# Squares turned by VectorE in the last batch, another tail and new orders of the steps: a fused attention and two-MoE kernel on one core

## The chip, the core and the metric

The kernel runs on one core of a Trainium2 chip. Its engines work side by side, each through its own queue in order: TensorE (PE: matmuls and transposes, its weight loads shown apart as PEld), VectorE (DVE), ScalarE (ACT), GpSimd (POOL) and SyncE (SP), which here issues all the transfers. The metric is the device time of one execution in microseconds.

## The reference

Three stages follow one another: attention with normalized queries and keys, a gated feed-forward layer, and a soft mixture of eight experts whose weights over tokens and slots come from the same logits.

```python
# attention: q, k, v of (4 batches, 12 heads, 448 tokens, 64)
q_n, k_n = rmsnorm(q, g_q), rmsnorm(k, g_k)
attn = softmax(q_n @ k_n.T / 8)
x = (attn @ v) as (1792 tokens, 768)
# gated layer, 768 -> 1536 -> 768
h = silu(x @ w_gate) * (x @ w_val)
x = h @ w_out
# soft mixture: phi (768, 32), 8 experts of 4 slots, hidden width 1024
logits = x @ phi
d = softmax(logits, over tokens);  c = softmax(logits, over slots)
slot_in = d.T @ x
slot_out[e] = relu(slot_in[e] @ w1[e]) @ w2[e]
return c @ slot_out
```

All is fp32. The rows of a token never meet those of another, but for the attention within a batch and the softmax over all 1792 tokens.

## The kernel before, in words

**Products in two parts.** A product of full accuracy is made of three faster ones: each operand is split into a high part (rounded, type fp32r) and a low part (what the rounding left), and high times high, high times low and low times high are summed. For the weights `w_hi` makes the high part on ScalarE and `w_lo` the low one (L239). Other products and all transposes stay fp32.

**Stages.** A hand-written schedule runs in steps `t`. In steps 0 to 27 (`step0`) the attention of batch 0 runs, with the preparation of the weights beside it: `w_out` times `phi` is folded into one matrix `wp`, so that the logits come straight from `h`, and the 24 blocks of `w_gate` and `w_val` are written back as fp32. From step 28 on (`step`, with `u = t - 28`) each step makes one product of 18 matmuls (`gv`, L615, in two halves `G0` and `G1`): even `u` a gate block, odd `u` the value block, so a pair gives one of the 12 blocks of 128 rows of `h` for a batch. The 24 steps of a batch carry the attention of the next batch with them; the last batch (`u` from 72 to 95) has no attention beside it.

**A block of `h`.** The gate goes through a tanh on ScalarE (`act_gate`), VectorE multiplies it (`act_gate_mul`, L636, then `act_val`, L642, with the value). The two products have one PSUM bank each (`g` and `v`), so a gate product can start only when the multiplication of the gate before has read its bank. Then the block is needed twice: as it is, for the logits (`logits`, `lp`, L679, summed by VectorE at L685, in the last batch for every two blocks), and with tokens on the partitions, for the slots. For that `h_trans` (L659) turns it on TensorE in four transposes of 112 tokens, and ScalarE copies the result from PSUM into `hn`.

**The end of a batch.** `slots1` sums the logits (`lt`) and makes them once more with tokens on the partitions (`ln`, L703 and L705, for `ce`); `slots2` takes the maximum and the exponential over tokens (`et`, with a running maximum over the batches); `slots3` turns `et` (`dp`, copied to `dn`), and `slots4` multiplies `dn` with `hn` (`sp`, L746) and adds to `acc`. For the last batch `slots4_last` goes on to the slots' inputs (`sip`).

**The experts.** From there the weights `w1` and `w2` of the experts stream through 15 buffers of 1.5 MB (`load_unit`); each unit of a load is consumed by 16 to 24 matmuls (`s` L1431 and `so` L1458). Loads wait in SP's queue for a buffer to come free; the first 11 are issued during the last batch. The last four units are ordered so that the left half of the 768 columns is ready first.

**The tail.** `combine1` to `combine3` make `c` (as `ct`, with high and low parts stacked, 96 rows). `slot_out` brings a half of the slots' outputs together: two copies out of PSUM, one matmul with a selecting matrix, a rounding and a subtraction (`sst`, 96 rows). `output` makes one matmul of 384 columns for 112 tokens (L1417) and one copy (L1419), VectorE and ScalarE by turns. `TO` says how many of the 16 output matmuls of the left half stand behind each of the last units: 8 before the right half's products, 8 between them.

**The order of a step** is written out as lists of names: `ORDA` for the first two steps, `ORD0` and `ORDB` for the rest of `step0`, `ORD1` for the first 24 of the later steps and `ORD2` for the others. `S` are the scores, `M0`/`M1` the maxima, `E0`/`E1` the exponentials, `P0`/`P1` the transposes of the probabilities and `V0`/`V1` their copies out of PSUM, `T`/`TH`/`L` the turning and splitting of queries and keys, `X` the product with `v`, `AT`/`AM` the activations, `HT` the turning of `h`, `LG` the logits, `W4` the split of the last batch's weights, `Z1` to `Z4` the `slots` functions. `fill(n)` issues 4n small matmuls on zeros, which keep TensorE at work (`warm_ps`, L115); `LF`, `TF` and `FILL` are their counts.

## Time and profile before

| | us |
|---|---|
| median of 3 runs | 833.52 |
| lowest and highest | 832.75, 835.16 |
| the profiled execution | 833.85 |
| its span | 832.1 |
| outside of the span | 1.75 |

The profile's page gives busy times by engine and the chain of waits that ended last: 60% of the span lies on TensorE, 33% in the products of L615, 6% in transfers of the experts' weights. TensorE's matmuls overlap: a product's matmul is shown with some 366 ns, and the next one starts 0.2 us later. What a group of matmuls costs is therefore read from the chain, where the time of a piece ends when the next one starts. Times on the left of a row are microseconds from the start of the span.

### The profile page before, as it was taken

The page shows a single profiled execution, that of the slowest core. Times are in us where ns is not written, and L with a number is a line of the kernel's source. Part 1 is how long each engine was busy: PE and PEld are TensorE (multiplying, and loading weights), DVE is VectorE, ACT ScalarE, POOL GpSimd, SP SyncE. Part 2 cuts the span into 40 slices and gives each one's busy share as a digit, 9 for nine tenths or more (in the row PEclk, how much of TensorE's full clock was granted, in tenths as well). Part 3 has the DMA queues.
Part 4 walks back from the last instruction along what each step waited for, and adds up shares of the span by engine and source line. Part 5 has one row for each costly group of instructions (what it writes and reads, how often), then busy time and mean ns, then how long its engine had stood idle before and what let it go on. Part 6 is the DMA issues. An engine that isn't in the chain of part 4 may idle for free.

```text
span 832.1 us, 14229 instructions
## 1 busy us (share of the span) xinstructions
PE 790.9 (95%) x5460; PEld 594.0 (71%) x5460; DVE 462.1 (56%) x777; ACT 439.3 (53%) x940; POOL 333.1 (40%) x327
## 2 busy tenths in 40 slices
PE   6799989999999999999999999999999999988685
PEld 5556657778778767787778677877878888555353
DVE  4879978777778555555556555545354344220013
ACT  3777877878678546556566455655333333220012
POOL 7987867675756543445444344322000000010000
PEclk8999999999999999999999999999999999999877
DMA  6566665765656312322223222221337778899997
GB/s 212 161 197 188 204 206 164 238 223 177 195 188 223 107 53 80 110 91 77 83 80 95 68 85 60 69 75 52 96 107 252 285 286 321 270 397 403 403 343 235
DMA packets 77891, 148.87 MB, mean 179 GB/s; under 512 B 5888, under 2 KB 48128, under 8 KB 77824
## 3 DMA queue, kind: packets, MB, share of 16 engines
q1 hardware_dynamic: 77824, 147.97, 53.5%
q8 instruction: 43, 0.70, 0.3%
q14 instruction: 24, 0.20, 0.1%
HBM read 128.29 MB, written 19.66 MB: 178 GB/s over the span
## 4 chain that ended last, share of the span: by engine, by line
PE 60%; DMA 6%; ACT 1%; POOL 1%; DVE 1%; issue 0%; SPq 0%; DVEq 0%; ACTq 0%; POOLq 0%
PE pg L615 33%; DMA w<-in_moe_w_dram 6%; PE tp L521 5%; PE xp L548 5%; PE s L442 3%; PE th L659 2%; PE so L1458 2%; PE sp L746 1%; PE lp L679 1%; PE tq L372 1%; PE s L446 1%; PE s L1417 1%; PE s L1431 1%; PE sip L800 0%; POOL pr L486 0%; PE ln L703 0%
## 5 line engine op out<-in xcount | busy, mean ns | idle before, releaser
L615 PE MATMUL pg<-xh,wh 128*128 128x448 f32 x576 | 222.5, 386 | 0.0
L615 PE MATMUL pg<-xl,wh 128*128 128x448 f32 x576 | 210.6, 366 | 0.0
L615 PE MATMUL pg<-xh,wl 128*128 128x448 f32 x432 | 157.9, 365 | 0.1
L457 DVE TENSOR_REDUCE sm<-s 128x1 f32<-128x448 f32 x168 | 100.5, 617 | 73.4 <-PE s L442 52.7
L469 ACT ACTIVATE pr<-s,sm 128x448 f32<-128x448 f32 x168 | 106.2, 639 | 63.5 <-DVE sm L457 61.1
L486 POOL TENSOR_SCALAR pr<-pr,su 128x448 f32<-128x448 f32 x84 | 70.9, 854 | 117.5 <-DVE su L482 106.0
L615 PEld LDWEIGHTS pg<-xh,wh 128*128 128x128 f32 x576 | 108.6, 189 | 12.4 <-issue 5.1
L615 PEld LDWEIGHTS pg<-xl,wh 128*128 128x128 f32 x576 | 108.9, 189 | 6.4
L521 PE MATMUL tp<-ident,pr 128*112 128x128 f32 x672 | 101.9, 280 | 4.3 <-ACT pt L535 2.1
L521 PEld LDWEIGHTS tp<-ident,pr 128*112 128x112 f32 x672 | 74.7, 135 | 38.2 <-issue 13.2
L231 ACT CAST wh<-raw 128x768 fp32r<-128x768 f32 x96 | 79.5, 830 | 29.0 <-PE pg L615 22.8
L239 DVE TENSOR_TENSOR wl<-raw,wh 128x768 fp32r<-128x768 f32 x72 | 81.0, 1124 | 11.2 <-ACT wh L231 11.2
L615 PEld LDWEIGHTS pg<-xh,wl 128*128 128x128 f32 x432 | 81.2, 188 | 7.2 <-DVE wl L239 0.5
L535 ACT COPY pt<-tp 112x512 f32<-112x512 f32 x130 | 74.0, 595 | 13.3 <-PE tp L521 7.4
L341 POOL TENSOR_TENSOR ri<-ss,mhalf 112x16 f32<-112x16 f32 (+1 forms) x25 | 70.1, 2805 | 2.1
L423 POOL CAST qz<-qa 64x128 fp32r<-64x128 f32 x48 | 35.1, 732 | 78.3 <-DVE qa L414 70.1
L442 PE MATMUL s<-ka,qa 64*128 64x448 f32 x432 | 63.6, 399 | 0.8 <-ACT qa L403 0.7
L660 ACT COPY hn<-th 112x512 f32<-112x512 f32 x48 | 28.4, 591 | 58.9 <-PE th L659 58.9
L548 PE MATMUL xp<-pt,vt 112*64 112x448 f32 x288 | 58.1, 546 | 0.0
L347 POOL TENSOR_TENSOR qn<-qk,ri 112x512 f32<-112x512 f32 x46 | 52.9, 1150 | 1.1
L615 PE MATMUL pg<-xh,raw 128*128 128x448 f32 x144 | 52.6, 366 | 0.0
L197 POOL TENSOR_SCALAR hpos<-r 128x768 uint16<-128x768 int16 x36 | 46.2, 1282 | 4.6 <-DMA r<-in_moe_w_gate_dram 1.7
(161 smaller groups left out, 1103.9 us busy)
## 6 DMA issues: line engine op xcount, KB each, us to landing
w<-in_moe_w_dram SPq DMA_DIRECT2D x25, 1536.0 KB, 10.6
raw<-w SPq DMA_DIRECT2D x72, 384.0 KB, 3.2
w<-raw SPq DMA_DIRECT2D x36, 384.0 KB, 2.9
r<-in_moe_w_out_dram SPq DMA_DIRECT2D x12, 768.0 KB, 5.1
r<-in_moe_w_gate_dram SPq DMA_DIRECT2D x12, 768.0 KB, 5.2
r<-in_moe_w_val_dram SPq DMA_DIRECT2D x12, 768.0 KB, 5.0
qk<-in_q_dram SPq DMA_DIRECT2D x24, 224.0 KB, 3.2
qk<-in_k_dram SPq DMA_DIRECT2D x24, 224.0 KB, 3.4
```

What stands on the lines that cost most here:

```text
L231: (nc.vector.tensor_copy if u - NO < NU and WH1 == "v" else nc.scalar.copy)(out=wh, in_=wst[u]["raw"])
L239: eng.tensor_tensor(out=wl, in0=wst[u]["raw"], in1=wst[u]["wh"].bitcast(F32), op=ALU.subtract)
L341: nc.gpsimd.tensor_tensor(out=ri, in0=ss, in1=mhalf[:, : len(ns)], op=ALU.pow)
L347: eng.tensor_tensor(out=st[i]["qn"][:, n].rearrange("p c h d -> p h c d"), in0=st[i]["qk"][:, n], in1=st[i]["ri"][:, n] .rearrange("p (h c ...
L442: nc.tensor.matmul(sc[j], qa[r, wt, c * P : (c + 1) * P], ka[r, mv, :], start=(n == 0), stop=(n == 2))
L457: nc.vector.tensor_reduce(out=d["sm"][:, j : j + 1], in_=d["sc"][j], axis=AX.X, op=ALU.max, negate=True)
L469: nc.scalar.activation(out=p, in_=d["sc"][j], func=AF.Exp, bias=d["sm"][:, j : j + 1], accum_out=st[i]["su"][:, c, j : j + 1])
L486: nc.gpsimd.tensor_scalar(out=p, in0=p, scalar1=su[:, j : j + 1], scalar2=1.0, op0=ALU.mult, op1=ALU.mult)
L521: nc.tensor.transpose(tp[:CP, ck * P : (ck + 1) * P], pr[:, ck * CP : (ck + 1) * CP], ident)
L535: eng(out=st[i]["pt"][j][:, :, c * P : (c + 1) * P], in_=tp)
L548: nc.tensor.matmul(xp[HD * j : HD * j + HD, :S], d["vt"][:, j, ck, :], d["pt"][j][:, ck, :], start=(ck == 0), stop=(ck == NC - 1),)
L615: nc.tensor.matmul(d[r], wt[:, P * c : P * c + P], mv, start=(c == 0 and n == 0), stop=(c == KD - 1 and n == 2),)
```

## The change

- **Squares (`h_squares`, `H0` to `H3`).** In the last batch the tokens are cut as 128, 128, 128 and 64 instead of four times 112. For its first 11 blocks `HT` does nothing; VectorE turns the block itself, in squares of 32 x 32, from `ht` straight into `hn`. One instruction takes 32 partitions of `ht` and writes 32 partitions of `hn`, 4 or 3 squares wide; 16 make a block. `H0` and `H1` (8 instructions) run in the step after the value block, `H2` and `H3` at the head of the next one. The twelfth block is turned by TensorE as before, with a copy by ScalarE and one by VectorE. GpSimd clears the unused half of the fourth chunk.
- **Low parts.** For the last batch `w_lo` runs on GpSimd.
- **Logits per token.** `ln` is gone. `slots2` copies the logits out of PSUM (`lr`, in the buffer of `lg`), and `slots3` turns them behind `et` with four transposes more; `acl` takes the buffer of `lg` last.
- **The tail.** `ct` holds four equal copies of `c`, 32 rows each, in fp32. `slot_out` is one copy of 64 x 192 out of PSUM. `output` makes two fp32 matmuls of 192 columns and 32 rows each, into two PSUM banks, and copies one by VectorE and the other by ScalarE. All 16 of the left half stand ahead of the right half's products.
- **Orders and warming matmuls.** All five lists are new. `LF[3]` (in front of `slots1` of the last batch) goes from 3 to 0, `TF` (behind the last units and in `slot_out`) to 0.

SP's queue has the same transfers in the same order.

```diff
+    def tok(b):
+        return [P] * (S // P) + [S % P] if b == B - 1 else [CP] * NC
     def hn_tile(u):
...
-            d["hn"][g] = hnp.tile([CP, NC, 512], F32, tag="hn", name="hn", bufs=3)
+            d["hn"][g] = hnp.tile([P, NC, 512], F32, tag="hn", name="hn", bufs=3)
+            if b == B - 1:
+                nc.gpsimd.memset(d["hn"][g][S % P :, NC - 1], 0.0)
...
+    SQ = 32
+    hts_ = {}
+    def h_squares(u, g):
+        hn, o = hn_tile(u)
+        hk = hts_[u][SQ * g : SQ * g + SQ]
+        for k in range(P // SQ):
+            m = (S // SQ - k + P // SQ - 1) // (P // SQ)
+            nc.vector.transpose(
+                out=hn[SQ * k : SQ * k + SQ, :m, o + SQ * g : o + SQ * g + SQ],
+                in_=hk.rearrange("p (c q) -> p c q", q=SQ)[:, k :: P // SQ],
+            )
...
     def slots1(b):
...
-        ln = pt_tile("ln")
-        for c in range(NC):
-            o, cs = ln[:CP, NS * c : NS * c + NS], slice(CP * c, CP * c + CP)
-            nc.tensor.matmul(o, lg[:, cs], stack[:n, 0, :], start=True, stop=one)
-            if not one:
-                nc.tensor.matmul(o, ht[:, cs], wp[:, KF - 1, :], start=False, stop=True)
     def slots2(b):
...
-        nc.vector.tensor_copy(out=ce[:, b], in_=d.pop("ln")[:CP, : NC * NS].rearrange("p (c s) -> p c s", c=NC))
...
+        d["lr"] = d["lg"][:NS]
+        (nc.vector.tensor_copy if LRE == "v" else nc.scalar.copy)(out=d["lr"], in_=lt[:NS, :S])
...
         def W4():
...
-                w_lo(wu(u + 1), nc.vector)
+                w_lo(wu(u + 1), nc.gpsimd)
...
+        def H_(g):
+            w = prev if g < 2 else u - 2
+            if w is not None and (B - 1) * NU <= w < B * NU - 1 and w % 2 == 1:
+                if g == 0:
+                    hts_[w] = bt[w // NU]["ht"][w % NU // 2]
+                h_squares(w, g)
...
-    LF = [4, 3, 2, 3]
+    LF = [4, 3, 2, 0]
...
-    TF, TO = [0, 0, 0, 0, 4, 4, 0], [0, 8, 16, 16]
+    TF, TO = [0, 0, 0, 0, 0, 0, 0], [0, 16, 16, 16]
...
         def slot_out(n):
...
-            for j in (2 * n, 2 * n + 1):
-                eng = nc.scalar.copy if j % 2 else nc.vector.tensor_copy
-                eng(out=sos[NS * j : NS * j + NS, DQ * j : DQ * j + DQ], in_=so[NS * j : NS * j + NS, :])
-            s3 = pt_tile("s3")
-            nc.tensor.matmul(s3[: 3 * NS, :384], sel[r], sos[r, cs], start=True, stop=True)
+            r = slice(2 * NS * n, 2 * NS * (n + 1))
             fill(TF[5 + n])
-            nc.scalar.copy(out=sst[n], in_=s3[: 3 * NS, :384])
-            sub_lo(sst[n][2 * NS :], s3[2 * NS : 3 * NS, :384], sst[n][2 * NS :])
+            (nc.scalar.copy if n else nc.vector.tensor_copy)(out=sos[r], in_=so[r, :])
         def output(n, i):
...
-            nc.tensor.matmul(op, ct[:, S * b + CP * c : S * b + CP * c + CP], sst[n], start=True, stop=True)
-            eng = nc.scalar.copy if c % 2 else nc.vector.tensor_copy
-            eng(out=ot[b][:, c, cs], in_=op)
+            ops = [(s_tile(k) if k < 3 else pt_tile("op"))[:CP, :DQ] for k in ((2 * i + j) % 6 for j in range(2))]
+            for j in range(2):
+                r = slice(NS * (2 * n + j), NS * (2 * n + j + 1))
+                nc.tensor.matmul(
+                    ops[j], ct[r, S * b + CP * c : S * b + CP * c + CP], sos[r], start=True, stop=True
+                )
+            for j, eng in enumerate((nc.vector.tensor_copy, nc.scalar.copy)):
+                eng(out=ot[b][:, c, DQ * (2 * n + j) : DQ * (2 * n + j + 1)], in_=ops[j])
```

The list of the main part of the first stage, of the five the one that the prediction speaks of:

```diff
     ORD0 = (
-        "M1 X TP M0 P0 R NA SS WT NB TH S U2 TL V0 WV P1 NC XM U CT C W2 XH E0 E1 V1 WE Q XL G2"
+        "X TP P0 M0 WT NB M1 R SS TH NA V0 S U2 P1 NC XM U WV CT TL E0 XH C V1 XL W2 G2 E1 Q WE"
```

What this makes of the queues is seen in three places. First VectorE in the last batch, before, from the logits sum of one pair of blocks (L685) over two blocks: gate multiplication (L636), value multiplication (L642) and the low parts between them.

```order
L685 TENSOR_TENSOR lg<-lp,lg 64x448
L636 SCALAR_TENSOR_TENSOR ht<-ht,pg 128x448
L239 TENSOR_TENSOR raw<-raw,wh 128x768
L642 SCALAR_TENSOR_TENSOR ht<-ht,pg 128x448
L239 TENSOR_TENSOR raw<-raw,wh 128x768
```

The same place after, from the logits sum (now L715) to the squares of the next block:

```order
L715 TENSOR_TENSOR lg<-lp,lg 64x448
L685 STREAM_TRANSPOSE hn<-ht 32x4x32 x2
L685 STREAM_TRANSPOSE hn<-ht 32x3x32 x2
L685 STREAM_TRANSPOSE hn<-ht 32x4x32 x2
L685 STREAM_TRANSPOSE hn<-ht 32x3x32 x2
L636 SCALAR_TENSOR_TENSOR ht<-ht,pg 128x448
L642 SCALAR_TENSOR_TENSOR ht<-ht,pg 128x448
L685 STREAM_TRANSPOSE hn<-ht 32x4x32 x2
```

The low parts have left the queue, and the second half of a block's squares stands between the logits sum and the next gate multiplication.

Second TensorE in the tail, before: the output matmuls (`s` and `op`, L1417) of the left half on either side of the products of the right half (`so`, L1458).

```order
L1417 MATMUL s<-w,ct 112x384 x3
L1417 MATMUL op<-w,ct 112x384 x2
L1417 MATMUL s<-w,ct 112x384 x3
L1458 MATMUL so<-w,h1m 32x192 x16
L1417 MATMUL op<-w,ct 112x384 x2
L1417 MATMUL s<-w,ct 112x384 x3
L1417 MATMUL op<-w,ct 112x384 x2
L1417 MATMUL s<-w,ct 112x384
L1458 MATMUL so<-w,h1m 32x192 x16
```

After, the last output matmuls of the left half (now L1450), the products of the right half (L1493) and its first output matmuls:

```order
L1450 MATMUL op<-sos,ct 112x192 x3
L1450 MATMUL s<-sos,ct 112x192 x2
L1493 MATMUL so<-w,h1m 32x192 x32
L1450 MATMUL s<-sos,ct 112x192 x3
L1450 MATMUL op<-sos,ct 112x192 x3
```

The two units' products now stand together, and nothing but one copy lies between them and the output matmuls.

Third ScalarE in the third step, the first with `ORD0`, before: the two exponentials (L469) stand together ahead of the copies of turned probabilities out of PSUM (L535).

```order
L405 CAST ka<-tq 128x448
L535 COPY pt<-tp 112x4x128
L469 ACTIVATE pr,su<-s,sm 128x448 x2
L535 COPY pt<-tp 112x4x128 x2
L253 COPY wot<-tw 128x384
```

After, the same step:

```order
L405 CAST ka<-tq 128x448
L535 COPY pt<-tp 112x4x128
L469 ACTIVATE pr,su<-s,sm 128x448
L535 COPY pt<-tp 112x4x128
L469 ACTIVATE pr,su<-s,sm 128x448
L535 COPY pt<-tp 112x4x128
L253 COPY wot<-tw 128x384
```

A copy now stands between the two exponentials.

## Rows read from the trace of the kernel before

**Rows 1.** The page: busy us, share and instructions of each engine.

```profile
PE 790.9 (95%) x5460; PEld 594.0 (71%) x5460; DVE 462.1 (56%) x777; ACT 439.3 (53%) x940; POOL 333.1 (40%) x327
```

**Rows 2.** Stretches: length, busy us of each engine, granted clock, DMA share, GB/s.

```profile
20.00:30.00 10.00, 6.38 (x44) 4.96 (x43) 7.90 (x13) 6.67 (x17) 9.38 (x9) 0.89 0.30 67
...
640.00:660.00 20.00, 20.00 (x103) 17.60 (x102) 8.43 (x11) 6.64 (x10) 0.00 (x0) 1.00 0.82 306
...
720.00:730.00 10.00, 9.29 (x80) 4.44 (x72) 2.48 (x8) 0.53 (x2) 0.00 (x0) 0.91 0.74 244
...
740.00:780.00 40.00, 34.03 (x622) 20.46 (x614) 5.55 (x18) 4.11 (x10) 4.02 (x11) 1.00 1.03 403
780.00:800.00 20.00, 13.74 (x106) 5.78 (x108) 0.51 (x4) 0.77 (x2) 0.00 (x0) 0.58 1.04 390
```

**Rows 3.** Waits of TensorE and its weight loads in the first stage: us, times, longest.

```profile
PE tp L521 <- ACT pt L535: 2.1, 1, 2.1
...
PEld tp L521 <- ACT pr L469: 7.9, 10, 1.5
```

**Rows 4.** All waits of TensorE's matmuls from 136 to 710 us.

```profile
PE tp L521 <- POOL pr L486: 0.5, 1, 0.5
```

**Rows 5.** Chain of waits, 298 to 307 us: start, time on the chain, what.

```profile
301.47 0.72 PE ln L703 x8
...
305.30 0.33 PE dp L736 x4
```

**Rows 6.** Chain of waits, one pair of blocks of the last batch.

```profile
648.78 0.88 PE lp L679 x4
649.66 5.67 PE pg L615 x27
655.33 0.43 PE th L659 x4
655.76 7.30 PE pg L615 x36
663.06 0.44 PE th L659 x4
```

**Rows 7.** Timeline of ScalarE and VectorE, last batch: start, duration, what, wait before it.

```profile
641.53 0.82 ACT L231 CAST wh<-raw 128x768 fp32r<-128x768 f32 x1
644.53 0.84 ACT L231 CAST wh<-raw 128x768 fp32r<-128x768 f32 x1 [2.18 <-PE pg L615]
...
653.34 0.84 ACT L231 CAST wh<-raw 128x768 fp32r<-128x768 f32 x1 [2.39 <-PE pg L615]
...
649.73 0.62 DVE L685 TENSOR_TENSOR lg<-lp,lg 64x448 f32<-64x448 f32 x1 [3.37 <-PE lp L679]
```

**Rows 8.** Groups by form, VectorE: busy us, mean ns of one, idle time before.

```profile
L784 DVE TENSOR_TENSOR acl<-acl,sp 128x384 f32<-128x384 f32 x2 | 1.1, 550 | 2.6 <-PE sp L746 2.6
...
L784 DVE TENSOR_TENSOR acl<-acl,sp 128x128 f32<-128x128 f32 x1 | 0.3, 289 | 0.1
```

**Rows 9.** Line 203 on GpSimd: shortest, median, longest in ns; first and last start.

```profile
L203 POOL TENSOR_TENSOR hpos<-hpos,hneg x11: 1814/1860/2122, 130.1 to 261.1; 128x768 f32<-128x768 f32 x11
```

**Rows 10.** Chain of waits behind the last product of the last batch.

```profile
711.92 0.69 PE warm_ps L115 x12
...
719.30 4.01 PE sp L746 x24
```

**Rows 11.** Chain of waits in the tail.

```profile
797.20 7.00 PE so L1458 x64
...
804.22 0.36 DVE sos L1403
...
809.02 2.72 PE so L1458 x32
...
819.33 0.78 PE s L1417 x3
```

**Rows 12.** Chain of waits, scores in the middle of the run.

```profile
371.97 0.80 PE s L442 x6
```

More of the change, by code (lines that the diff above doesn't have):

```diff
@@ L657, in h_trans @@
         th4 = pt_tile("th4")
-        for c in range(NC):
-            nc.tensor.transpose(th4[:CP, P * c : P * c + P], ht[:, CP * c : CP * c + CP], ident)
-        nc.scalar.copy(out=hn[:, :, o : o + P], in_=th4[:CP, :].rearrange("p (c f) -> p c f", c=NC))
+        t0 = 0
+        for c, n in enumerate(tok(b)):
+            nc.tensor.transpose(th4[:n, P * c : P * c + P], ht[:, t0 : t0 + n], ident)
+            t0 += n
+        th4 = th4.rearrange("p (c f) -> p c f", c=NC)
+        if b < B - 1:
+            nc.scalar.copy(out=hn[:CP, :, o : o + P], in_=th4[:CP])
+        else:
+            n = S % P
+            nc.scalar.copy(out=hn[:, : NC - 1, o : o + P], in_=th4[:, : NC - 1])
+            nc.vector.tensor_copy(out=hn[:n, NC - 1, o : o + P], in_=th4[:n, NC - 1])
+    SQ = 32
[9 more added lines that the diff above has]
+            )
+        if g == P // SQ - 1:
+            del hts_[u]
     def logits(u):
@@ L734, in slots3 @@
         dp = pt_tile("dp")
-        for c in range(NC):
-            nc.tensor.transpose(
-                dp[:CP, NS * c : NS * c + NS], d["et"][:NS, CP * c : CP * c + CP], ident[:NS, :NS]
-            )
-        d["dn"] = mp.tile([CP, NC, NS], F32, tag="dn", name="dn", bufs=1)
-        nc.vector.tensor_copy(out=d["dn"], in_=dp[:CP, : NC * NS].rearrange("p (c s) -> p c s", c=NC))
+        d["dn"] = mp.tile([P, NC, NS], F32, tag="dn", name="dn", bufs=1)
+        if b == B - 1:
+            nc.gpsimd.memset(d["dn"][S % P :, NC - 1], 0.0)
+        for n, (src, dst, ck) in enumerate(((d["et"], d["dn"], tok(b)), (d["lr"], ce[:, b], [CP] * NC))):
+            o = dp[:, NC * NS * n : NC * NS * (n + 1)].rearrange("p (c s) -> p c s", c=NC)
+            t0 = 0
+            for c, m in enumerate(ck):
+                nc.tensor.transpose(o[:m, c], src[:NS, t0 : t0 + m], ident[:NS, :NS])
+                t0 += m
+            if n == 0 and b == B - 1:
+                nc.vector.tensor_copy(out=dst[:, : NC - 1], in_=o[:, : NC - 1])
+                nc.vector.tensor_copy(out=dst[: ck[-1], NC - 1], in_=o[: ck[-1], NC - 1])
+            elif b < B - 1:
+                nc.vector.tensor_copy(out=dst[:CP], in_=o[:CP])
+            else:
+                nc.scalar.copy(out=dst[:CP], in_=o[:CP])
     def slots4_mul(b, g):
@@ L851, in combine3 @@
             nc.tensor.transpose(
-                cp[: 3 * NS, CP * c : CP * c + CP], c3[:, c].rearrange("p i s -> p (i s)"), ident[:CP, :CP]
+                cp[:, CP * c : CP * c + CP], c3[:, c].rearrange("p i s -> p (i s)"), ident[:CP, :CP]
             )
-        cb = ct[:, S * b : S * b + S]
-        evac_hi(cb, cp[: 3 * NS, :S])
-        sub_lo(cb[NS : 2 * NS], cp[NS : 2 * NS, :S], cb[NS : 2 * NS])
+        nc.scalar.copy(out=ct[:, S * b : S * b + S], in_=cp[:, :S])
     KD2, KH2 = KD // 2, KH // 2
@@ L1383, in attn_moe_softmoe_kernel @@
         warm_tag[0] = "v"
[L1384 to L1386 removed]
+        ct = tp_.tile([P, NT], F32, name="ct")
+        sos = tp_.tile([P, DM // 4], F32, name="sos")
         so = ps.tile([P, 192], F32, tag="g", name="so")
```

36 lines of the change are left out of this document (13 added, 23 removed).

## The prediction

> **What bounds the kernel now.** The page first: TensorE's matmuls fill 95% of the span, VectorE, the next engine, 56% [rows 1]. A busy TensorE can still wait, so the table by stretches comes next, and it shows three stages [rows 2]. Up to about 136 us TensorE idles in places (6.4 us busy of 10 from 20 to 30 us); who it waits for there is the list of waits [rows 3]. From 136 to 710 us the same list holds one wait of 0.5 us [rows 4]: the stage is bound by what stands in TensorE's queue, so a piece of TensorE work taken out is time gained, and a new order of the steps can gain next to nothing. From about 730 to 800 us the DMA engines are full (share 1.03 and 1.04) and TensorE waits for the weights of the experts [rows 2]. After that comes a tail in which TensorE, the copies out of PSUM and the output transfers follow one another [rows 11].
>
> The full DMA stretch doesn't swallow what is gained ahead of it: it starts when the last batch gives its buffers back, the bytes after that don't change, and in the last batch the DMA engines have a share of 0.82 [rows 2]. Over the 100 us of that batch 18 us are free, so the same loads fit into 5 us less.
>
> **The change, part by part.**
>
> *Transposes of the last batch off TensorE.* In the last batch (612 to 712 us) each of 11 blocks loses four transposes, 0.43 to 0.44 us on the chain [rows 6]: 11 x 0.435 = 4.8 us. A pair of blocks takes 7.30 + 5.67 + 1.82 for the products, 0.88 for the logits and twice 0.435 [rows 6], 16.54 us (the 1.82 is a quarter of the 7.30); without the transposes a block is 7.84 us of TensorE. The twelfth block stays on TensorE. ScalarE's copy of each block goes too, off the path.
>
> *The same turned by VectorE.* 16 instructions per block, 8 of 128 elements per partition and 8 of 96. No row shows such an instruction. The nearest are plain two-input ones: 550 ns for 384 elements, 289 ns for 128 [rows 8], so 1.02 ns for an element and 158 ns to start, 256 ns for 96: 16 cost 4.4 us. The lower end is elements alone, 16 x 0.115 = 1.8 us; the upper end, if each element passes twice, 420 and 354 ns, 6.2 us. I take 4.4, 0.272 for one. Per block VectorE keeps two multiplications and half a logits sum (0.62 each [rows 7]), 1.55, and gives the two low parts away: 5.9 of 7.84 us, no bound. The tight place is its queue behind the logits sum of every second block, since the second half of a block's squares stands there ahead of the gate's multiplication, which frees the PSUM bank that TensorE needs next. Before, the sum ends at 649.73 + 0.62 = 650.35, and TensorE is through with the other product at 653.34, when ScalarE's next split is released by it [rows 7]. Of these 2.99 us the multiplication takes 0.62 and the signal some 0.04 (an estimate from the gaps between instructions in the chain): eight squares have 2.33 us, 0.29 each. At 0.272 they fit; the term is 0, and nothing is left over for a surprise.
>
> The Trainium skill speaks against this part: its page "VectorE: DVE Perf Modes" (Rules for kernel authors) gives a full 128x128 turn to TensorE where PSUM will do as destination, and its section on the three transpose paths puts VectorE at 311 ns for 128 columns in squares of 32, which no run here shows. By 311 ns for each of the sixteen, eight would take 2.49 us, 0.16 too much at five places, and the sum below would be 10.0 instead of 10.8 us.
>
> *Low parts on GpSimd.* The same shape with two inputs took GpSimd 1.81 to 2.12 us, 1.86 in the middle, between 130 and 261 us, beside a busy VectorE [rows 9]. In the last batch GpSimd is idle [rows 2]. The high part ends at 641.53 + 0.82 = 642.35; the low part then at 644.2 to 644.5. TensorE is through with the unit before at 644.53 and needs the low part two matmuls later, 0.4 us [rows 7]. So it is hidden up to a price of about 2.6 us; each 0.1 us above costs 24 times 0.1. Three memsets and a small copy stand in the same queue, and with 1.9 of 4.1 us per unit in use they fit. The term is 0.
>
> *Logits per token.* The eight matmuls "ln" of a batch (0.72 us) give way to four transposes like "dp" (0.33) [rows 5]; for the three earlier batches 3 x 0.39 = 1.2 us. The copies that come with them lie on VectorE, for which TensorE doesn't wait in that stage [rows 4].
>
> *From the last product to the slot sums.* 711.92 to 719.30 us [rows 10]. Twelve warming matmuls ahead of it go (0.69). The "ln" group of the last batch goes from TensorE, but the exponential doesn't wait for it; on VectorE a copy of the last block's rest now stands ahead of the maximum, and a copy of the logits (as long as the 0.62 sum) ahead of that of dn. Taken together a gain of 0.4, between a gain of 1.7 and a loss of 1.5: the slot sums take 4.01 us [rows 10] in a stretch with a granted clock of 0.91 on the mean [rows 2], and could take less or stay.
>
> *The tail.* The first half's last product ends at 797.20 + 7.00 = 804.20, and the first output matmul of the second half starts at 819.33 [rows 11]: 15.1 us. After the change one copy (0.36) follows 804.20; then 32 output matmuls in pairs, all ahead of the second half's products. Such a pair, 192 columns in fp32 in two tiles of the array, costs what one of the "so" pairs costs: 16 matmuls in 2.72 us [rows 11], 0.34 for a pair, 5.4 for sixteen. Two copies out of PSUM per pair go to two engines and take no longer (0.36 for 192 columns). Then twice 2.72 for the products, one copy of 0.4 with its signals: 804.6 + 5.4 + 5.4 + 0.4 = 815.9 instead of 819.33, 3.4 us gained; the warming matmuls, two copies, a matmul, a rounding and a subtraction are what left the path. The rest to the end, bound by the output transfers, moves with it. Without the warming matmuls the clock could fall again: 64 "so" records take 7.00 us behind a stretch granted 0.58, between the levels of 1.2 and 2.4 GHz, and twice 2.72 later [rows 2, 11], so the products would lose 1.6 us; TensorE has work without a gap there, and the term stays, with this in the range.
>
> *New orders.* In the 136 us at the start TensorE's own order within a step of the main part is unchanged; on ScalarE a copy out of PSUM moves ahead of the second exponential. Waits of the first kind are what the list shows: 2.1 us for a copy, 7.9 us of weight loads for an exponential [rows 3]. I take 1.0 us of gain, between 4 gained and 3 lost. From 136 to 710 us: 0, between 1 and -2. SP's queue keeps its order, so no transfer moves against another.
>
> **Sum:** 4.8 + 1.2 + 0.4 + 3.4 + 1.0 = 10.8 us. The profiled run took 833.85 (span 832.1, 1.75 around it): 823.05. It lies 0.33 above the median of the three runs, 833.52, so 822.7.
>
> **Rivals.**
>
> *A. The squares are dearer than 0.29 us.* At 0.387 (the upper end) eight take 3.10, 0.77 too much at five places (the sixth logits sum has no gate behind it): 3.9 us given back, 826.6. For it: the operation is in no row. Against: nothing says that it passes elements twice.
>
> *B. The output matmuls of 32 rows don't overlap.* Then a pair costs 0.68 and the first half 5.4 us more; in the second half the extra 5.4 hides in part behind the output transfers, say 2 remain: 830.1. For it: no row has two tiles of 32 rows. Against: tiles of 64 rows do overlap, six half-height matmuls of 448 columns take 0.80 us [rows 12], where of full height 36 take 7.30 [rows 6], 1.22 for six. The Trainium skill's page "TensorEngine Tiling (Array Packing)" (Key Properties) has tiles of 32 rows run in parallel too; by it B falls away and its 7.4 us with it; no run here shows it.
>
> *C. VectorE becomes the bound of the last batch, slower than before.* A block then takes 16 p + 1.55 us. It passes TensorE's 7.84 at p = 0.39, and the whole gain of 10.8 is gone at p = 0.455. If a square costs two plain instructions (0.578 and 0.512, mean 0.545) a block takes 10.27, 11 x 2.43 = 26.7 us more: 849.4.
>
> *D. The orders open new waits* in the tight first stage: 3 us lost instead of 1.0 gained, 826.7; much more would be needed for a loss overall.
>
> *E. The DMA queue doesn't follow* and eats the gain ahead of 730 us (7.4): 830.1. The share of 0.82 speaks against it.
>
> **How the numbers follow.** Forecast 0.58 (819 to 826), A 0.10, B 0.11, C 0.06, D 0.12, E 0.03. About 0.3% (2.5 us) is what a measurement here can tell from no change, so "faster" ends at 831.0. A is faster; of B 0.05 faster and 0.06 the same; of D 0.09 faster, 0.02 the same, 0.01 slower; C slower; E faster: 0.85, 0.08, 0.07. The range, 817 to 830, takes in the better ends of the orders and of the slot sums below, and A, D and most of B above; C and a part of the rest stay out.
>
> **What would show it.** In the profile after: a block of the last batch takes 7.84 us on the chain with no gap between products; squares at 0.2 to 0.29 us; GpSimd's low parts at 1.8 to 2.1 us; the DMA engines full from about 723 us; 11.7 us from the end of the first half's product to the second half's first output matmul. It is wrong if products wait for the gate's multiplication behind the logits sums (A, C), if the two matmuls of an output pair start 0.3 us apart (B), or if TensorE's idle time in the first 136 us grows (D).

## The result and the profile after

The changed kernel takes 824.89 us (median of 4, 824.29 to 825.7) against 833.93 (median of 4): a ratio of 0.9891, with a 95% interval of 0.9875 to 0.9908. It is 9.0 us faster; 822.7 was forecast, with a range of 817 to 830. The profiled execution took 825.70 (span 823.9), 8.15 less than the one before, where the sum had 10.8.

The engine line of the page after, to be held against [rows 1]: TensorE has 9.4 us less work, VectorE 22.6 and GpSimd 53.6 us more.

```profile
PE 781.5 (95%) x5440; PEld 584.0 (71%) x5440; DVE 484.7 (59%) x943; ACT 434.8 (53%) x943; POOL 386.7 (47%) x354
```

The chain of waits of the kernel after, at the marks where one stage gives way to the next (start, us on the chain, what):

```profile
608.76 0.89 PE lp L709 x8
...
705.97 1.24 PE pg L615 x6
...
726.33 0.59 ACT si L1413
...
796.19 2.81 PE so L1493 x32
...
805.13 5.35 PE so L1493 x64
...
810.87 0.74 PE s L1450 x5
```

Two of the same marks in the kernel before that no group shows yet:

```profile
610.76 0.89 PE lp L679 x8
...
731.39 0.59 ACT si L1370
```

The first logits sum of slots ("lt") marks the end of the first batch's way; of this row of the tile's list the first start is what counts (300.6 before, 298.8 after):

```profile
L696 PE MATMUL lt<-lg,stack x8: 537/537/639, 300.6 to 713.0; 128*128 128x448 f32 x6, 64*128 64x448 f32 x2
```

```profile
L726 PE MATMUL lt<-lg,stack x8: 536/537/640, 298.8 to 707.6; 128*128 128x448 f32 x6, 64*128 64x448 f32 x2
```

From mark to mark, the before side from these rows and [rows 10, 11]:

| stretch | before | after | gain | forecast |
|---|---|---|---|---|
| start to first "lt" | 300.6 | 298.8 | 1.8 | 1.0 (orders) |
| to the logits at 610.76 / 608.76 | 310.2 | 310.0 | 0.2 | 0.8 (two batches' "ln") |
| to the end of the last product, 711.92 / 707.21 | 101.2 | 98.5 | 2.7 | 5.2 (squares 4.8, "ln" 0.4) |
| to the slot inputs, 731.39 / 726.33 | 19.5 | 19.1 | 0.35 | 0.4 |
| to the first half's last product, 804.20 / 799.00 | 72.8 | 72.7 | 0.14 | 0 |
| to the second half's first output matmul, 819.33 / 810.87 | 15.1 | 11.9 | 3.26 | 3.4 (tail) |
| to the end of the span, 832.1 / 823.9 | 12.8 | 13.0 | -0.26 | 0 |

Of the first half's last products only the ends are compared, 804.20 and 799.00: behind the mark at 797.20 [rows 11] stand the 64 of both last units, behind that at 796.19 the 32 of the last one.

The gain ahead of 730 us reaches the end: the DMA stretch takes as long as before, only earlier. Its first part in the windows of the kernel after (columns as in [rows 2]):

```profile
720.00:730.00 10.00, 8.71 (x96) 5.08 (x92) 0.36 (x1) 1.68 (x4) 0.00 (x0) 1.00 0.99 351
```

The DMA share from 720 to 730 us is 0.99, where it was 0.74 [rows 2]: the queue follows. What is missing lies in the last batch and at the slots. There the chain shows one pair of blocks at 0.88 + 15.29 = 16.17 us, against 16.54 before [rows 6] and the 15.68 (twice 7.84) of the forecast; from 629.50 to 693.71, over four pairs, it is 16.05 on the mean.

```profile
645.44 0.88 PE lp L709 x4
646.32 15.29 PE pg L615 x72
```

VectorE at the tight place of that pair, from its timeline (start, duration, operation, wait ahead):

```profile
646.39 0.62 DVE L715 TENSOR_TENSOR lg<-lp,lg 64x448 f32<-64x448 f32 x1 [1.52 <-PE lp L709]
647.02 2.39 DVE L685 STREAM_TRANSPOSE hn<-ht 32x128 f32<-32x128 f32 x8
649.44 0.62 DVE L636 SCALAR_TENSOR_TENSOR ht<-ht,pg 128x448 f32<-128x448 f32 x1
```

And TensorE's timeline beside it. The products follow one another every 0.21 us; behind the last product of a unit comes a gap of 0.35:

```profile
649.86 0.37 PE L615 MATMUL pg<-xh,raw 128*128 128x448 f32 x1
650.21 0.44 PE L615 MATMUL pg<-xh,wh 128*128 128x448 f32 x1
```

The gate's multiplication ends at 649.44 + 0.62 = 650.06, and the product that needs its bank starts at 650.21, 0.15 later. Without the wait it would have started at 650.07. The profile names no releaser for this wait; that it is the gate's multiplication is shown by the second experiment.

At the slots of the third batch a stretch of 1.2 us stands on the chain (614.04 to 615.25) in which TensorE makes no more than four small transposes and then waits 0.6 us:

```profile
612.42 1.62 PE pg L615 x8
614.04 0.19 ACT sml L748
...
614.25 0.22 DVE ssum L749
614.47 0.52 DVE lg L754
614.99 0.21 DVE dn L773
...
615.25 0.40 PE dp L767 x4
```

In the kernel before, products ran there on either side of the small transposes:

```profile
617.04 0.33 PE dp L736 x4
617.37 2.02 PE pg L615 x9
619.39 2.71 PE sp L746 x24
```

Three causes were put to the test: the late gate multiplication, the slow succession of the products (0.2067 us in this pair, 0.2027 in others), and the stops at the slots. So were the squares, the low parts, the tail and the first orders by themselves; the logits per token and the new main order were not. All times below are medians; the kernel before had 833.9 to 834.1 beside them. Two slow executions are left out of them, one of 1528.63 us (transposes back on TensorE) and one of 2509.85 us (old orders).

### The profile page after: what moved, and what is told of

It reads as the page before. It is cut to its first block, busy times and chain, and to the rows that moved or that the text cites. A ratio compares the mean times of both kernels' runs of the same rounds, so it can differ in the third digit from the quotient of the medians.

```text
span 823.9 us, 14472 instructions
## 1 busy us (share of the span) xinstructions
PE 781.5 (95%) x5440; PEld 584.0 (71%) x5440; DVE 484.7 (59%) x943; ACT 434.8 (53%) x943; POOL 386.7 (47%) x354
## 4 chain that ended last, share of the span: by engine, by line
PE 85%; DMA 6%; POOL 2%; ACT 2%; DVE 2%; issue 1%; SPq 0%; DVEq 0%; POOLq 0%; ACTq 0%
PE pg L615 43%; PE tp L521 9%; PE xp L548 7%; PE s L442 6%; DMA w<-in_moe_w_dram 6%; PE tq L372 3%; PE s L548 2%; PE th L666 2%; PE so L1493 2%; PE s L446 2%; PE lp L709 2%; PE sp L782 1%; PE s L1466 1%; PE s L1450 1%; PE tw L247 1%
## 5 line engine op out<-in xcount | busy, mean ns | idle before, releaser
L486 POOL TENSOR_SCALAR pr<-pr,su 128x448 f32<-128x448 f32 x84 | 80.4, 966 | 139.9 <-ACT pt L535 62.5
L469 ACT ACTIVATE pr<-s,sm 128x448 f32<-128x448 f32 x168 | 107.6, 643 | 11.0 <-DVE sm L457 10.8
L535 ACT COPY pt<-tp 112x512 f32<-112x512 f32 x130 | 75.4, 590 | 66.0 <-PE tp L521 59.9
L521 PE MATMUL tp<-ident,pr 128*112 128x128 f32 x672 | 103.6, 277 | 2.5 <-ACT pt L535 1.8
L239 DVE TENSOR_TENSOR wl<-raw,wh 128x768 fp32r<-128x768 f32 x72 | 74.4, 1034 | 8.3 <-ACT wh L231 8.3
L239 POOL TENSOR_TENSOR raw<-raw,wh 128x768 fp32r<-128x768 f32 x24 | 44.2, 1842 | 69.3 <-ACT wh L231 67.1
L341 POOL TENSOR_TENSOR ri<-ss,mhalf 112x16 f32<-112x16 f32 (+1 forms) x25 | 72.8, 2911 | 2.1
L629 ACT ACTIVATE ht<-pg 128x448 f32<-128x448 f32 x48 | 26.1, 544 | 70.9 <-PE pg L615 45.9
L347 POOL TENSOR_TENSOR qn<-qk,ri 112x512 f32<-112x512 f32 x46 | 59.1, 1286 | 1.1
L442 PEld LDWEIGHTS s<-ka,qa 64*128 64x128 f32 x432 | 35.5, 187 | 27.3 <-issue 24.3
```

What stands on the lines that cost most here:

```text
L239: eng.tensor_tensor(out=wl, in0=wst[u]["raw"], in1=wst[u]["wh"].bitcast(F32), op=ALU.subtract)
L341: nc.gpsimd.tensor_tensor(out=ri, in0=ss, in1=mhalf[:, : len(ns)], op=ALU.pow)
L347: eng.tensor_tensor(out=st[i]["qn"][:, n].rearrange("p c h d -> p h c d"), in0=st[i]["qk"][:, n], in1=st[i]["ri"][:, n] .rearrange("p (h c ...
L442: nc.tensor.matmul(sc[j], qa[r, wt, c * P : (c + 1) * P], ka[r, mv, :], start=(n == 0), stop=(n == 2))
L469: nc.scalar.activation(out=p, in_=d["sc"][j], func=AF.Exp, bias=d["sm"][:, j : j + 1], accum_out=st[i]["su"][:, c, j : j + 1])
L486: nc.gpsimd.tensor_scalar(out=p, in0=p, scalar1=su[:, j : j + 1], scalar2=1.0, op0=ALU.mult, op1=ALU.mult)
```

## The experiments

**Transposes back on TensorE.** The squares are left out, and the blocks of the last batch go through TensorE again:

```diff
-                elif prev < (B - 1) * NU:
+                else:
                     h_trans(prev)
...
-            if w is not None and (B - 1) * NU <= w < B * NU - 1 and w % 2 == 1:
+            if False and w is not None and (B - 1) * NU <= w < B * NU - 1 and w % 2 == 1:
```

> The changed kernel, but the h blocks of the last batch go back to TensorE: four transposes a block, copies by ScalarE; everything else stays. Baseline of the changed kernel: 824.9 us, of the kernel before: 833.9. Eleven blocks get back 0.435 us each of TensorE, 4.8 us. Theory one (the squares delay the gate's multiplication, about 1.1 us over the batch, and the long runs of products without transposes fall into a slower cadence, 206.6 ns from product to product instead of 202.7, about another 1.1 us): both go with the squares, the mean pitch is 203 ns again from 640 to 710 us, and the time is 824.9 + 4.8 - 2.2 = 827.5. Rival one (the slow cadence comes from the low parts on GpSimd, which stay): pitch 206 in parts, 828.6. Rival two (neither the waits nor the cadence belong to the squares): 829.7.

828.43 us, ratio 0.9946 (0.9928 to 0.9964). The squares are worth 3.5 us as they stand in the changed kernel; by these intervals a difference of some 2 us between two kernels is at the edge of the noise, so the time alone doesn't tell 3.5 from 4.8. The time lies between theory one's 827.5 and rival one's 828.6 and doesn't choose between them. The chain says more: the slow succession is there without a square. Two groups of 36 products of this kernel, 206 and 203 ns each, neither with a wait in it:

```profile
658.36 7.43 PE pg L615 x36
...
675.07 7.30 PE pg L615 x36
```

But this profiled execution is not a typical one: it took 835.08 us, the longest of its kernel, and its granted clock is 0.95 from 640 to 700 us, where the changed kernel and the next one have 1.00:

```profile
640.00:700.00 60.00, 60.00 (x307) 52.47 (x306) 12.46 (x25) 18.80 (x30) 28.63 (x17) 0.95 0.80 285
```

The fast group stands at the same 0.95, so the clock alone doesn't make the slow one; whether it has a part in it, no other profile of this kernel can say. That squares bring the slow succession with them is thus put in doubt, not disproved. Rival one falls further below: with the low parts back on VectorE the slow succession is there as well.

**Gate's multiplication first.** One move in the main order:

```diff
-        "H2 H3 X S NB Z3 T AT NC M0 AM XM ...
+        "X S NB Z3 T AT NC M0 AM H2 H3 XM ...
```

> The changed kernel with one move: the gate's multiplication stands ahead of the second half of the squares in VectorE's queue, instead of behind. Theory one: the waits of 0.15 to 0.2 us between the 18th and 19th product of a run, six places, go away: about 1.0 us, 823.9, pairs of blocks 15.95 us on TensorE with the slow cadence; if the cadence is then also the fast one, pairs of 15.68 and 822.8. Rival (TensorE doesn't wait for the gate's multiplication there): nothing moves, 824.9. Against a gain: the squares then stand right ahead of the value's multiplication, 2.4 us in some 2.4 of room.

823.42 us, ratio 0.9875 (0.9855 to 0.9894), 1.5 less than the changed kernel; the two intervals overlap, so the time alone decides little. In its profile the pairs take 15.66 us, what the forecast had for the squares done right:

```profile
643.77 0.88 PE lp L709 x4
644.65 14.78 PE pg L615 x72
```

The 14.78 for 72 products are the 7.30 + 5.67 + 1.82 that they took in [rows 6]; no gap and no slow succession is left in the batch. Theory one holds, and by the pairs its better branch. The time lies between the two branches (822.8 and 823.9); in the profile the slot sums of the last batch take 4.41 us, where the changed kernel has 3.58. Against the first experiment the squares are now worth 5.0 us.

**Slots apart.** Z3 (the small transposes) moves behind the first half of the products, Z4 (slot sums), HT and the first squares behind the second:

```diff
-        "H2 H3 X S NB Z3 T ... W4 M1 Z4 XL ... WH G0 NA Z1 CT E1 HT H0 H1 N0 ... G1 WL R LG V1 Q C"
+        "H2 H3 X S NB T ... W4 M1 XL ... WH G0 Z3 NA Z1 CT E1 N0 ... G1 Z4 HT H0 H1 WL R LG V1 Q C"
```

> The changed kernel with one move in the order of the main steps: the transposes of the slot weights (dp) behind the first half of a step's products, and the slot sums (sp) behind the second half, so that products stand between them as before the change. Theory: the stop between 614.0 and 615.7 us, where TensorE has only dp and sp to do and waits for the exponential, the logits' copy and dn's copy, goes: about 0.9 us, 824.0. Rival (the wait moves to the release of a PSUM bank or of an hn buffer): no change, 824.9. The two earlier batches have the same steps beside attention; a loss there would show as a time above 824.9.

836.33 us, ratio 1.0029 (1.0015 to 1.0044): 11.4 us slower than the changed kernel, slower than the kernel before. In the last batch this is rival C of the prediction in one place. All sixteen squares of the first block queue up behind the accumulation of the slot sums, and the gate's multiplication stands behind them:

```profile
628.75 4.77 DVE L685 STREAM_TRANSPOSE hn<-ht 32x128 f32<-32x128 f32 x16
633.55 0.62 DVE L636 SCALAR_TENSOR_TENSOR ht<-ht,pg 128x448 f32<-128x448 f32 x1
```

TensorE waits 2.5 us for it. More is lost earlier: from the first "lt" to the logits of the third batch this kernel takes 317.5 us (297.4 to 614.86), the changed one 310.0. Since HT moved too, ScalarE's copy of the turned `h` now stands six times ahead of a copy of turned probabilities, and TensorE's product with `v` waits for both, 5.2 us in all. The first time:

```profile
321.84 0.58 ACT hn L670
322.42 0.28 ACT pt L537
```

As a test of the stop at 614 us the run is spoiled.

**The tail alone.** The kernel before with combine2, combine3, slot_out and output of the changed kernel, and without the warming matmuls of the tail:

```diff
-    TF, TO = [0, 0, 0, 0, 4, 4, 0], [0, 8, 16, 16]
+    TF, TO = [0, 0, 0, 0, 0, 0, 0], [0, 16, 16, 16]
```

> The kernel before with the new tail alone: combine weights in fp32 for four groups of 32 rows, one copy of the slot outputs instead of copies, select matmul and split, two output matmuls of 32 rows per block of tokens, all sixteen pairs of the first half ahead of the second half's last products, no warming matmuls. Theory: the way from the end of the first half's last product to the second half's first output matmul falls from 15.1 to 11.9 us as in the changed kernel, some 0.3 of it is lost among the output transfers: 833.9 - 2.9 = 831.0. Rival (part of the tail's gain hangs on the earlier start of the last stage in the changed kernel): 15.1 falls by under 2 us, 832 or more. If the first half's last products run at the lower clock as before the change, the second half's may too (1.4 to 2.7 us more).

831.11 us, ratio 0.9965 (0.995 to 0.998): 3.0 us, as expected. The way from the first half's last product (802.11 + 2.81 = 804.92) to the second half's first output matmul is 11.86 us:

```profile
802.11 2.81 PE so L1448 x32
...
811.05 5.35 PE so L1448 x64
...
816.78 0.74 PE s L1405 x5
```

**Old orders in the first part.** The changed kernel with ORD1, ORDA, ORD0 and ORDB as they were:

```diff
-        "AT NB Z3 X W4 S NC XM NA SP T AM WH P0 Z1 TH G0 M0 M1 L WL E0 CT E1 N0 P1 ...
+        "NA X Z1 W4 NB S NC T SP WH AT M1 P0 P1 XH M0 TH AM CT G0 Z2 XL L Z3 E1 E0 N0 G1 ...
```

> The changed kernel with the old orders of the steps in the first 136 us (the three orders of the stage ahead of the products and that of the first batch's steps); the main order stays new. My term for the new orders was 1.0 us of gain, between 4 gained and 3 lost. If it holds, 824.9 + 1.0 = 825.9. Rival one (the new orders only move the waits about: by the gaps between TensorE's instructions the first 136 us have 27.2 us of idle time before and 27.5 after): 824.9, within 0.5. Rival two: the old order with the new first part costs more, since the copy out of PSUM stands behind the second exponential again (waits of 2.1 and 7.9 us): up to 828.9.

828.07 us, ratio 0.9931 (0.9913 to 0.995): the new orders are worth 3.2 us to the changed kernel, where the sum had 1.0. That is within rival two's bound of 828.9, and 2.2 above the 825.9 of the term. The first product starts at 127.6 and the first "lt" at 302.1 us:

```profile
L726 PE MATMUL lt<-lg,stack x8: 536/537/640, 302.1 to 711.2; 128*128 128x448 f32 x6, 64*128 64x448 f32 x2
```

**New orders in the first part, alone.** The opposite edit: the kernel before with the four new orders.

> The kernel before with the new orders of the steps in the first 136 us and the first batch alone. Theory one (these orders are the term that I had at 1.0 us and that the changed kernel with the old ones put at some 4): first logits sum of slots (the lt matmul of the first batch) near 298.2 us instead of 301.8, the means over profiles of each kind, and 834.0 - 3.6 = 830.4. Rival one (the orders pay only together with the new main order): 833 or more. Rival two (the term of 1.0 was right and the changed kernel with old orders lost for another reason): 833.0.

831.86 us, ratio 0.9968 (0.9956 to 0.9981): 2.2 us, between theory one (3.6) and rival two (1.0). The first "lt" is at 298.4 us.

Taken together: 2.2 and 3.2 us by the times, 3.8 by the means of the profiles. Three profiles with the old orders have the first "lt" at 300.6, 302.1 and 302.8 us, eleven with the new ones between 297.3 and 300.4, 298.1 on the mean. The profiled execution of the kernel before, at 300.6, is the quickest of its kind here, which is why it made the orders look like 1.8 us in the table.

**Low parts on VectorE.** The changed kernel with one word back:

```diff
-                w_lo(wu(u + 1), nc.gpsimd)
+                w_lo(wu(u + 1), nc.vector)
```

> The changed kernel with the weights' low parts of the last batch back on VectorE, beside the squares. A block of the last batch then holds on VectorE 16 x 0.298 (squares) + 2 x 0.622 (multiplications) + 0.31 (half a logits sum) + 2 x 0.96 (low parts) = 8.25 us against 7.84 of TensorE. Theory one (VectorE becomes the bound of the last batch): at least 11 x 0.41 = 4.5 us more, 829.4, and TensorE stops for the gate's multiplication or the low part in every block. Rival (the queue has enough slack in front, the first blocks have it): under 2 us more, 826.9.

827.72 us, ratio 0.9927 (0.9913 to 0.9942): 2.8 us more, between the two. In the last batch the chain now runs on VectorE, through squares, the multiplications and the low part, and TensorE comes after it:

```profile
656.64 0.62 DVE ht L636
657.26 0.88 DVE raw L239
...
658.19 3.52 PE pg L615 x16
```

From logits to logits it is 16.7 us, 0.3 more a block than the 16.05 of the changed kernel on the mean; the estimate of 0.41 counted from a TensorE without gaps. So the move to GpSimd is what keeps the squares from being the bound. The slow succession is in this profile too: from 639.94 to 641.18 seven products start 0.2067 us apart, and elsewhere they start 0.203 apart. The low parts on GpSimd are not needed for it.

**Without squares.** VectorE writes zeros instead (the slot sums miss eleven blocks):

```diff
-                nc.gpsimd.memset(d["hn"][g][S % P :, NC - 1], 0.0)
+                nc.vector.memset(d["hn"][g], 0.0)
...
-        for k in range(P // SQ):
+        for k in range(0):
```

> The changed kernel without the squares of the last batch: VectorE writes zeros into the transposed h instead (three memsets), so the last batch's slot sums miss eleven of twelve blocks; all else stays. What the squares still cost. Theory one (they cost by the late gate multiplication alone, and with it go the waits and the slow cadence, as in the kernel with the gate's multiplication first): pairs of blocks of 15.66 us, 202.6 ns from product to product, 823.4. Rival one (the slow cadence has nothing to do with squares or waits): no waits of 0.15 us, but runs with 206.6 ns, 823.9 to 824.4. Rival two (squares also cost elsewhere, at the end of the last batch): under 822.9.

823.37 us, ratio 0.9869 (0.9854 to 0.9884), the number of theory one, and the same as the kernel with the gate first. Its pairs, 0.88 + 14.79 us, are those of the gate first too. Behind the gate's multiplication, sixteen squares a block cost TensorE nothing that can be measured.

**Small transposes together.** Gate first, and in slots3 all eight small transposes ahead of both copies:

```diff
                 nc.tensor.transpose(o[:m, c], src[:NS, t0 : t0 + m], ident[:NS, :NS])
                 t0 += m
+        for n, (src, dst, ck) in enumerate(((d["et"], d["dn"], tok(b)), (d["lr"], ce[:, b], [CP] * NC))):
+            o = dp[:, NC * NS * n : NC * NS * (n + 1)].rearrange("p (c s) -> p c s", c=NC)
             if n == 0 and b == B - 1:
```

> The kernel with the gate's multiplication first, and the eight small transposes of a batch (four of the slot weights, four of the logits) issued together ahead of the two copies, instead of each four with its copy. In the trace of the changed kernel the second four start when the first four's copy has ended, 0.37 us of stop in each of the two earlier batches and some 0.6 in the third. Theory one (they wait for that copy because both share a tile): 2 x 0.37 + 0.5, 1.2 us less than 823.4: 822.2. Rival (the slot sums then wait for the copy of dn instead, which stands right ahead of them in time): 823.4, or 823.0.

821.35 us, ratio 0.9848 (0.9834 to 0.9862), 2.1 us less; but not for the reason given. The stop is still there in the first batch's slots, the slot sums have it now, as the rival said:

```profile
302.19 0.56 PE dp L767 x8
...
302.77 0.30 DVE dn L775
...
303.21 2.78 PE sp L784 x24
```

What differs in the two profiles is the last batch's slot sums: 2.71 us here, 4.41 in the kernel with the gate first, whose granted clock is 0.50 from 711.76 to 713.76 us, where it is 1.00 here. The next run is about this.

**Warming matmuls in the idle time.** The changed kernel with 48 instead of 12 ahead of the last "dp":

```diff
-    LF = [4, 3, 2, 0]
+    LF = [4, 12, 2, 0]
```

> The changed kernel with 48 warming matmuls instead of 12 ahead of the last batch's slot weights (dp), where TensorE stands idle for 3.6 us after the last transposes; 48 take 2.8 us (12 took 0.69). Theory one (that idle time is what lets the granted clock fall to 0.5 two us later, so the slot sums take 3.6 to 4.4 us instead of 2.7): slot sums 2.71 us with the clock at 1.00, 0.9 to 1.7 us less: 823.2 to 824.0. Rival (the clock falls there anyway, as it did in the profiled run of the kernel before, where TensorE had no idle time ahead): slot sums 3.6 or more, 824.9. Should the warming matmuls delay dp, it is up to 0.5 us slower.

823.20 us, ratio 0.9868 (0.9853 to 0.9883): 1.7 less. Windows of the changed kernel behind its last "lt" (length, PE, PEld, DVE, ACT, POOL, granted clock, DMA share, GB/s); TensorE works 0.41 of 2 us, and then the clock is at 0.50, its lower level of 1.2 GHz:

```profile
711.14:713.14 2.00, 0.41 (x5) 0.31 (x5) 1.00 (x4) 0.89 (x3) 0.00 (x0) 0.96 1.02 410
713.14:715.14 2.00, 2.00 (x16) 1.40 (x20) 0.00 (x0) 1.40 (x5) 0.00 (x0) 0.50 0.91 369
```

The same two stretches with 48 warming matmuls, the clock at 1.00 throughout, and the slot sums on the chain:

```profile
709.81:711.81 2.00, 1.42 (x25) 1.21 (x22) 1.00 (x4) 0.90 (x3) 0.00 (x0) 1.00 1.01 400
711.81:713.81 2.00, 2.00 (x24) 1.14 (x28) 0.00 (x0) 1.57 (x5) 0.00 (x0) 1.00 0.91 369
```

```profile
712.75 2.71 PE sp L782 x24
```

The slot sums take 2.71 instead of 3.58, and what follows them in the next 2 us is at full clock too: theory one's numbers, though a gain of 1.7 us is at the edge of the noise. All three profiles with 48 warming matmuls here have 2.71; of the eight with 12, seven have 3.58 to 5.06. The idle time isn't the whole of it. The eighth, the one with the small transposes together, kept 1.00 and 2.71 us behind a stretch in which TensorE worked 0.67 of 2 us, and the kernel before lost its clock at the same place (4.01 us of slot sums, [rows 10]) with a TensorE that its windows show as busy.

**All of it.** Gate first, small transposes together, 48 warming matmuls, the last copy of the logits on ScalarE:

> Gate's multiplication first, the eight small transposes together, 48 warming matmuls ahead of the last slot weights, and the last batch's copy of the logits on ScalarE instead of VectorE. From 821.35: the copy on ScalarE takes up to 0.53 us out of the chain ahead of the slot weights; the warming keeps the clock in those executions in which it fell: 820.3 to 821.3. Rival (the logits' copy on ScalarE ends later, behind the small exponential, and the four transposes of the logits wait for it): 821.4 or above.

822.15 us, ratio 0.9866 (0.9845 to 0.9887), nothing gained over 821.35: the clock had held there already, and the logits' copy on ScalarE is worth nothing that can be measured; in its profile the 48 warming matmuls stand on the chain themselves (2.68 us), so what a shorter copy would give doesn't show. And with the slot sums behind the first half of the products:

```diff
-        ... W4 M1 Z4 XL P0 V0 E0 L SP WH G0 NA Z1 ...
+        ... W4 M1 XL P0 V0 E0 L SP WH G0 Z4 NA Z1 ...
```

> As the kernel before it in this call, and the slot sums moved behind the first half of a step's products, where they stood before the change, with the transposes of h behind them as now. Theory one (in three batches the slot sums then find dn copied, so a stop of some 0.35 us goes in each): 1.0 us less. Rival (the accumulation of the slot sums on VectorE and sixteen squares queue up ahead of the gate's multiplication in the last batch, as in the kernel with the slots apart, which stopped TensorE for 2.5 us): 1 to 2 us more, with a wait of products for the gate's multiplication in the first block of the last batch.

819.36 us, ratio 0.983 (0.9814 to 0.9845), 5.5 us less than the changed kernel and 14.7 less than the one before. It is 2.8 less than without this move, where 1.0 was expected; in the two profiles the way from the first "lt" to the last product is 1.3 us shorter (406.5 and 405.2), and the rest stays open. Now the stop at the first batch's slots is gone, since products stand between the small transposes and the slot sums:

```profile
301.70 0.55 PE dp L767 x8
...
302.83 1.80 PE pg L615 x9
304.64 2.71 PE sp L784 x24
```

At the third batch's slots TensorE still waits for the logits' copy. The rival didn't come: with the gate ahead of the second half of the squares the last batch's pairs stay at 0.88 + 14.79 us.

## Why the prediction was right, and where it was off

The sign, the size and the range held, but partly because two errors cancelled: the squares and the slots gave less than the sum had, the orders more.

**Squares (4.8 forecast; 3.5 by the run without them, 2.7 by the chain, five and a half pairs at 16.54 and 16.05).** The step that failed is "At 0.272 they fit; the term is 0", by two sizes. A square takes 0.298 us from start to start (eight take 2.39; 0.30 us of work for 128 columns, 0.27 for 96), so eight take 0.21 more than forecast. And "the signal some 0.04" is 0.15 here, from the end of the gate's multiplication to TensorE's product (650.06 to 650.21), so eight squares had 2.99 - 0.62 - 0.15 = 2.22 us, 0.278 each, and not 0.29. At 0.298 TensorE is 0.16 late: rival A on a small scale, at every pair, as the prediction's own rule has it. With the forecast price the squares would have fitted into 2.22; with the forecast signal they would have been 0.05 late. The 0.15 isn't a price of the two engines everywhere: VectorE's copy of the slots' outputs ends at 799.38, and the first output matmul starts at 799.42. The Trainium skill's page "VectorE: DVE Perf Modes" (The three transpose paths) gives VectorE 311 ns for 128x128 elements of bf16 in squares of 32; the prediction took this for one instruction, and the 0.30 of this trace lies near it, though it is for fp32 and 32 partitions. The rest is the slow succession of the products, 0.28 us in a pair that has it throughout (72 times 4 ns), which no term had.

**Low parts on GpSimd (0).** Right: 1.84 us on the mean, hidden. The prediction gave the move no worth of its own, though it named VectorE's load with and without it; taken back, it costs 2.8 us.

```profile
L239 POOL TENSOR_TENSOR raw<-raw,wh 128x768 fp32r<-128x768 f32 x22 | 40.5, 1841 | 50.6 <-ACT wh L231 48.4 <-DVE lg L754 2.2
```

**Logits per token (1.2 forecast, about nothing).** The instructions cost little more than was said (0.40 for four, 0.33 forecast), but the step that the copies lie "on VectorE, for which TensorE doesn't wait in that stage" was wrong in the new order, where small transposes and slot sums follow each other without products between. The rows above show TensorE waiting for the logits' copy, then dn's. A wait list of the old order [rows 4] can't vouch for a new one. No run has this part by itself; an estimate is what the others leave of the 9.0 us: tail 3.0, squares 3.5 and first orders 2.2 to 3.2 make 8.7 to 9.7, which leaves this part and the new main order about nothing.

**From the last product to the slot inputs (0.4 forecast, 0.35 by the profiles).** Right by luck of the two executions: in both the granted clock fell, and without the slot sums (4.01 and 3.58) the way is 15.5 us in either. Where the clock held, this way was 1.4 us or more shorter. The prediction had the clock in this term's range, but not that 3.6 us in which TensorE has only 12 warming matmuls and four small transposes (709.55 to 713.12) would stand ahead of the slot sums.

**Tail (3.4 forecast, 3.0 alone).** Right. Sixteen pairs of output matmuls take 799.42 to 805.13, 5.7 us (5.4 forecast), and rival B falls: matmuls of neighbouring groups of 32 rows start 0.16 us apart and last twice that:

```profile
799.84 0.32 PE L1450 MATMUL op<-sos,ct 32*112 32x192 f32 x1
800.00 0.32 PE L1450 MATMUL s<-sos,ct 32*112 32x192 f32 x1
```

This is also what the page "TensorEngine Tiling (Array Packing)" of the Trainium skill (Key Properties) says of different tiles of the array: they can run matmuls in parallel.

**Orders (1.0 forecast, 2.2 to 3.8).** The mis-sized term, within the bounds given for it. Its first step, TensorE's own order unchanged, holds for the main part of the first stage, but not in the first batch's steps from 126 us on: there P1's four transposes now stand between the two halves of the products, while before all eight stood together. For these steps the sum had 0 ("a new order of the steps can gain next to nothing"), and that failed: from the first product to the first "lt" it is 302.1 - 127.6 = 174.5 us with the old orders and 298.8 - 126.0 = 172.8 with the new, in two kernels that differ in them alone at that point. All three profiles with the old orders have 174.5 to 174.7, the ten with the new ones at full clock 172.7 to 172.9. Of these 1.8 us the wait of 0.5 [rows 4] is one part, gone with the new orders; the rest isn't taken apart here.

```profile
L615 PE MATMUL pg<-xh,wh x576: 358/368/718, 127.6 to 710.0; 128*128 128x448 f32 x192
```

```profile
L615 PE MATMUL pg<-xh,wh x576: 360/368/718, 126.0 to 706.4; 128*128 128x448 f32 x192
```

**Rivals C, D and E.** VectorE is the bound only with the low parts back on it (and at one place with the slots apart), D has the wrong sign, and the DMA queue follows the batch.

**Open:** what makes a group of products succeed at 206.7 instead of 202.7 ns. At a granted clock of 1.00 it was seen in the five profiles in which the squares stand ahead of the gate's multiplication, though not in every pair of them, and in none of the other eight: five with the gate first or without squares, three with the old main order. Against a late gate as the whole cause stands the one group of the first experiment, without squares, at 0.95. No run tried it by itself.

## What to carry to other kernels

Work moved to an engine with room must also find room in that engine's order: put what releases the busy engine's buffer ahead of the moved work. Here the moved work then cost nothing that could be measured (823.42 with it, 823.37 without). Where two dependent small steps are drawn together in the order, look for what filled the time between them, and put it back. Take the price of a signal from the very place that is tight; 0.1 us in the signal and 0.2 in the price of eight squares, met in every pair of blocks, decided this one. And look at the granted clock of a profile before its rows are held against another's.

## What the runs showed that was not expected

Matmuls of one shape and one clock succeed each other at 202.7 or at 206.7 ns for whole groups of 36, in one and the same execution. The idle stretch of TensorE ahead of the last slot sums cost twice in seven of eight profiles: the wait, and 0.9 to 2.4 us more for the slot sums at a lower granted clock behind it. And the first product comes after 124.5 to 126.1 us with the new orders, 125.9 to 128.2 with the old, so one profiled execution doesn't settle a term of 2 us there.
